# LSH attention and gMLP on one core: k of fifteen pairs turned by VectorE instead of TensorE

## The chip, the cores and the metric

The kernel runs on one core of one Trainium2 chip. The metric is the device time of one execution in microseconds (us), given as the median of several runs. The profile is of one further execution on the same chip, and its times are counted from the first instruction of the program.

## The reference

The inputs q, k and v have 4 batches, 8 heads, 768 rows and 64 columns, in float32. First comes an attention with hashed buckets: each row of q and of k gets a six-bit bucket from the signs of its product with `proj`, and a query sees only the keys of its own bucket.

```
q_bits = (einsum('bhsd,dk->bhsk', q, proj) > 0);  k_bits likewise
mask   = q_bucket[:, :, :, None] == k_bucket[:, :, None, :]
scores = where(mask, (q @ k^T) / sqrt(D), -1e9);  attn = softmax(scores)
x      = heads of (attn @ v) side by side            # 4 x 768 x 512
```

Then a gated MLP works on x: `h = gelu(x @ w_in)`, split into u and v; v is normalised, multiplied by `g_ln`, mixed over the rows by `w_sg`, and gets `b_sg` added; the output is `x + (u * v_s) @ w_out`.

## The kernel before

**The work.** The 32 heads are taken two at a time as 16 pairs, numbered n = 0 to 15. One pair needs q and k transposed: 64 columns of either head on the partitions (128 for both heads) and the 768 rows along the free dimension. Products have float32 accuracy because each operand is kept as a high part `h` (rounded to the fast format) and a low part `l` (the rest), and three products are added up: hi*hi, lo*hi and hi*lo.

**Loading and splitting a pair (what the change touches).** `load` (line 467) issues two DMAs for q and two for k on the queue of SyncE, called SP here (k of the first pair goes over ScalarE's queue). The tile has six blocks of 128 rows; a row of a head is 64 values, 256 bytes in the tile. q is loaded in blocks of 128 consecutive rows, k with six consecutive rows on each partition (`"(p t) d -> p t d"`), so the keys come in a permuted order, and `values` (line 495) loads v in the same order. The tiles for raw q and k are rings of two (`RAWS`), so that the load of a pair waits until the tile of the pair two before has been read. `parts` (line 505) then makes the transposed operands in three chunks of 512 columns, for each of which TensorE (PE in the profile) does four 128x128 transposes into PSUM (line 516), ScalarE (ACT) copies the high part (line 520) and a full copy `x` (line 529), and VectorE (DVE) subtracts the high part from PSUM to give the low part (line 523). For pair 1 alone the subtraction is done by GpSimd (POOL, line 531). A pair thus costs twelve transposes on PE, six for q and six for k.

**The rest of a pair.** `bits` (line 555) gets the sign features from `x` (PE line 563, DVE line 566, four small DMAs at line 572). `largest` (line 576) computes scores for the row maxima (PE line 591), which DVE reduces (lines 599 and 601). `shift` (line 605) carries the maxima by small DMAs into the feature tile `f` (line 618). `weigh` (line 623) computes the scores again with features and maxima (PE line 643), ACT takes the exponential (line 648), POOL adds up the row sums (line 678), and PE multiplies by v (lines 666 and 669, written `av`). `finish` (line 683) sends the sums through DRAM (lines 708 to 714), DVE inverts them on the way (line 710), and POOL and DVE scale the result (lines 721 and 722), which goes to DRAM. Beside the pairs run 16 weight jobs (line 324, DVE lines 343 to 350), which turn `w_in` into the form that the MLP needs.

**The MLP stage.** Its products are at lines 918, 1187 and 1233; on the way operands are split by ACT and by DVE or POOL (lines 895, 896, 902, 903, 1216 and 1217). Which of the two engines subtracts is listed in the constants `lox`, `loz`, `log` and `low`. `gate_raw` (line 976) and `residual` (line 1195) load in runs of 128 bytes into 32 partitions at a time and let DVE transpose 32x32 blocks (lines 984 and 986, 1203 and 1205).

**The order of the work.** Nothing is executed in the order of the source text. Every step is put into `Plan` (line 51) with an engine, an estimated cost, a priority (a due time, from constants such as `PREP`, `BITP`, `LATEQ`), and the tiles that it reads and writes. `Plan.order` simulates the engines and the SP queue with these costs and emits one fixed order; each engine, the SP queue too, then works strictly in that order. `split` (line 759) and `prepare` (line 764) place the splitting of pair n+1 some two pairs ahead of its use, and `maxima` runs `AHEAD` = 8 units ahead of `weigh` (a pair has nine units). While too little is ready at the start, PE is kept busy by 30 filler products (line 757).

Of the kernel before, what the change touches and what calls it, by code (L numbers as in the profile page):

```python
# [9 lines left out]
F32 = mybir.dt.float32  # L10
# [8 lines left out]
DRAM = bass.MemoryType.DRAM  # L19


MX = {'r0n': 3, 'zn': 2.99, 'base': 340.0, 'gs': False, 'norm': 'ACT', 'mul': ('DVE', 'DVE', 'POOL', 'DVE', 'DVE', 'POOL', 'POOL', 'DVE'), 'wg': -9.83, 'z0': -2.89, 'ox': -66.33, 'oz': -9.96, 'sp': -11.83, 'ro': -13.35, 'gr': -3.94, 'lx': 4.73, 'lz': -3.11, 'gap': 11.25, 'wo': -42.48, 'ws': 7.61, 'ul': 26.67, 'wi': -132.86, 'x0': -110.0, 'lox': ('POOL', 'DVE', 'POOL', 'POOL', 'DVE', 'DVE', 'DVE'), 'loz': ('POOL', 'DVE', 'DVE', 'DVE', 'POOL', 'POOL', 'POOL'), 'log': ('POOL', 'DVE', 'DVE', 'POOL'), 'low': ('DVE', 'DVE', 'POOL', 'DVE', 'DVE', 'DVE', 'DVE'), 'grb': 1, 'wob': 1, 'wj': -38.13}

AVP = 9.1
TRIP = 1.5
PRP, RAWS, LATEQ, PRQ = -24.5, 2, 4.39, True
GY, GX, NPT = (3,), (3, 3), 14
NAV = 1
S0P = 0.76
AHEAD = 8  # L30
PREP, SHIFTP, FINP, WSTEP, WP = 0.43, -0.07, 3.42, 14.6, 16.57
LOADS = "SP"
ADDS = (["POOL", "POOL"], ["POOL", "POOL", "POOL", "POOL", "POOL"])
TAILP = -1.15
FIRSTP, FIRSTS, FIRSTQ, LATE = -3.35, 3.76, -5.62, 11.08
LOAD0 = 1.35
PARTP = 0.39
OPS = 3
# [3 lines left out]
AHEAD1 = 2.82  # L42
LOP = (1,)
LATS, XS = (1.4, 2.6, 1.8, 3.2), 0.8
BITP, BITL, FZP, XB = -16.85, 4.0, 0.97, 1
JOB0, JOBS, JOBL = 1, 108, 6.0
LOADW = 7.8
SHIFTL = 3.2

# [1 line left out]
class Plan:  # L51
# [10 lines left out]
    TURN = 4.7  # L62
    STAY = 1.44
    BACK = 6.5
    SIDE = 1.8
    LAND = 0.62
    TAIL = {"DVE": 0.075, "ACT": 0.1, "POOL": 0.06}

    class Buf:
# [55 lines left out]
    def order(self):  # L125
# [32 lines left out]
        while len(out) < len(G):  # L158
# [44 lines left out]
            if g["dma"] and g["c"] > 1 and not g["lat"]:  # L203
                end = dma_free = max(dma_free, start + 0.6) + self.TURN
                seq[e] = max(start + 3.6, end - 1.5)
                end += 0.3 + self.LAND
                lanes.append(end + self.WAIT)
            elif g["lat"]:

                seq[e], end = end, start + g["lat"] + self.LAND  # L210
                lanes.extend([end + self.WAIT] * max(1, round(g["c"] / 0.57)))
            elif g["dma"]:
                seq[e] = end
                end = dma_free = max(dma_free, start + (1.38 if e == "ACT" else 1.3 if g["c"] > 1 else 1.2)) + g["dma"]
                end += 0.75 + self.LAND
                lanes.append(end + self.WAIT)
# [34 lines left out]
def kernel(  # L251
# [16 lines left out]
    nc = tc.nc  # L268

    B, H, S, D = q.shape  # L270
    P = 128
    NT = S // P
# [19 lines left out]
    PHASES = ((0, NY), (NY, S))  # L292
# [5 lines left out]
    ident = const.tile([P, P], F32, name="ident")  # L298
# [53 lines left out]
    PE, DVE, ACT, POOL, SP = "PE", "DVE", "ACT", "POOL", "SP"  # L352
# [4 lines left out]
    plan = Plan()  # L357
# [69 lines left out]
    if True:  # L427
# [5 lines left out]
        def ps_tile():  # L433
            ps_s.list.append(plan.slot(ps_slots, lambda i: ps_s.pool.tile([P, 512], F32, tag=f"g{i}",
                                                                          name=f"g{i}_{len(ps_s.list)}", bufs=1)))
            return ps_s.list[-1]

        def dma(prio, us, fn, r=(), w=(), e=SP, lat=0.0):
            eng = nc.sync if e == SP else nc.scalar
            plan.add(e, 0.6 if e == ACT else 0.57, prio, lambda: fn(eng), r, w, dma=us, lat=lat)  # L440
# [26 lines left out]
        def load(n, prio):  # L467
            st = Pair()
            st.n, st.b, st.hp = n, *divmod(n, NP)
            st.raw = []  # L470
            for s, (nm, src) in enumerate((("q", q), ("k", k))):
                t = early.ring([P, NT, 2, D], F32, nm, RAWS)
                for ts in ((slice(0, 2), slice(2, NT)) if n + s == 0 else (slice(0, NT),)):
                    for j in range(2):
                        def fn(eng, t=t, j=j, src=src, ts=ts):
                            order = "(p t) d -> p t d" if src is k else "(t p) d -> p t d"
                            eng.dma_start(t()[:, ts, j, :], src[st.b, 2 * st.hp + j].rearrange(order, p=P)[:, ts])
                        cost = 0.95 if s else 1.2 if n else LOAD0 * (ts.stop - ts.start) / NT
                        dma(prio + 0.2 * s + (LATEQ if ts.start else 0), cost, fn, w=[(t, (ph, j)) for ph in range(2) if ts.start <= 2 * ph < ts.stop],
                            e=ACT if n == 0 and s else LOADS)  # L480
                st.raw.append(t)
            if n == 0:
                warm = late.ring([P, 1], F32, "warm")
                plan.add(ACT, 1.4, prio + 0.5, lambda: nc.scalar.mul(warm(), small, 1.0), [], [warm])
            i = (NPAIR - 1 - n) % 3
            pool = (even, odd, early)[i]
            st.hi, st.lo = (pool.ring([P, 2, S], F32R, f"{a}{i}") for a in ("h", "l"))
            st.ft = plan.buf(f"f{i}", 1, lambda _, i=i: ftiles[i])
            pool.list.append(st.ft)
            st.x = early.ring([P, 2, S], F32, "x", XB) if n else None  # L490
            if n in (1, 2):
                plan.add(POOL, 1.5, prio + FZP, lambda t=st.ft: nc.gpsimd.memset(t().bitcast(F32), 0.0), [pnb], [st.ft])
            return st

        def values(st, prio):
            n = st.n
            st.v = pt.ring([P, 2, NT, D], F32, "v", 2)
            dma(prio + 2 if n else VP, 1.1, lambda eng: eng.dma_start(
                st.v(), v[st.b, 2 * st.hp:2 * st.hp + 2].rearrange("j (p t) d -> p j t d", t=NT)),
                r=[] if n else [(st.lo, (0, 0))], w=[st.v], e=LOADS)  # L500
        def chunk(i):
            (a, b), (c, d) = PHASES
            return ((slice(0, 2), slice(a, b), [(0, 0), (1, 0)]), (1, slice(c, d), [(1, 1)]), (0, slice(c, d), [(0, 1)]))[i]

        def parts(st, i, prio):

            hh, lo, (ss, cs, keys), tp = st.hi, st.lo, chunk(i), ps_tile()

            def at(t):
# [218 lines left out]
        sts, NPAIR = {}, B * NP  # L728
# [29 lines left out]

        def split(n, p0):
            sts[n] = load(n, p0 - (8 if n != 1 else AHEAD1))  # L760
            for i in range(3 if n else 2):
                parts(sts[n], i, p0 + 0.1 * i)

        def prepare(n):
# [30 lines left out]
        for n in range(NPAIR):  # L795
            for c in range(NU):
                if c == 0:
                    prepare(n + 1)
                g = NU * n + c
# [9 lines left out]

    M_ = MX  # L810
    V = nc.vector
# [433 lines left out]
    wi = in_weights(T + M_["wi"], T)  # L1245
# [63 lines left out]
```

## Time and profile before

| | |
|---|---|
| median of 3 runs | 699.15 us (698.44 to 699.97) |
| the profiled execution's own time | 698.67 us |
| its span, first to last instruction | 696.7 us |
| attention stage (last `av` product ends) | about 403.5 us into the span |
| MLP stage | from there to the end |
| busy: PE, DVE, ACT, POOL | 99%, 73%, 55%, 56% |

The time of a run is a little longer than the span (698.67 against 696.7 us), since starting and ending the program lie around it. PE's busy time is modelled from pipelined products, so a busy PE is one that has a product in flight. The chain of waits follows the work that ended last back through what released it. "SPq" is the queue of SyncE that issues the DMAs.

### The profile page before, as it was taken

To read this page: it belongs to the slowest core of one execution; us is meant where nothing else is said; L and a number is where in the kernel's file an instruction comes from. 1 tells how busy PE (TensorE), PEld (TensorE's weight loads), DVE (VectorE), ACT (ScalarE), POOL (GpSimd) and SP (SyncE) were. 2 spreads that over 40 slices of the span, in tenths; PEclk is the share of its full clock that TensorE was granted. 3 is DMA by queue.
4 is the path that set the end of the run, shared out by engine and by line. 5 is a ranking of instruction groups with operands and counts; after the bars stand their busy time and mean duration, and the time that the engine had idled before them with its cause. 6 is when DMAs were issued, how large, how long until landed. Compare 5 with 4: busy or idle time off the path is not lost.

```text
span 696.7 us, 16709 instructions
## 1 busy us (share of the span) xinstructions
PE 686.4 (99%) x6318; PEld 549.6 (79%) x6318; DVE 508.2 (73%) x949; ACT 380.3 (55%) x734; POOL 391.2 (56%) x346
## 2 busy tenths in 40 slices
PE   8999999999999999999999989999999999999997
PEld 8668666766766676676667579999999989899996
DVE  6878787787788769777778596786867965666343
ACT  3466666566766666676667656675774513242010
POOL 3477879777976977797679733261441514041030
PEclk9999999999999999999999999999999999999999
DMA  8524443443344334322242117888746584755433
GB/s 189 109 48 104 125 111 98 105 109 79 110 125 113 88 105 116 98 79 70 69 126 57 40 38 236 244 226 253 246 167 213 101 231 104 196 140 121 114 68 106
DMA packets 183124, 88.44 MB, mean 127 GB/s; under 512 B 148460, under 2 KB 162436, under 8 KB 183044
## 3 DMA queue, kind: packets, MB, share of 16 engines
q1 hardware_dynamic: 179940, 86.58, 46.2%
q10 hardware_dynamic: 3104, 0.80, 0.5%
q8 instruction: 50, 0.82, 0.5%
q14 instruction: 30, 0.25, 0.1%
HBM read 59.48 MB, written 25.36 MB: 122 GB/s over the span
## 4 chain that ended last, share of the span: by engine, by line
PE 91%; DMA 3%; DVE 2%; ACT 1%; issue 1%; POOL 1%; SPq 1%; ACTq 0%; DVEq 0%; POOLq 0%
PE g L643 18%; PE g L918 16%; PE g L1187 14%; PE av L666 11%; PE g L1233 9%; PE g L591 9%; PE av L669 5%; PE g L516 3%; PE g L699 2%; PE g L563 1%; PE ftp L757 1%; DMA sq<-s 1%; DMA f<-m 1%; POOL sum L678 1%; DMA r<-sq 0%
## 5 line engine op out<-in xcount | busy, mean ns | idle before, releaser
L648 ACT ACTIVATE p<-g 128x512 f32<-128x512 f32 x288 | 156.3, 599 | 60.3 <-PE g L643 58.5
L678 POOL TENSOR_TENSOR sum<-sum,p 128x512 f32<-128x512 f32 x152 | 178.3, 1206 | 3.8 <-ACT p L648 3.5
L599 DVE TENSOR_REDUCE mx<-g 128x1 f32<-128x512 f32 x192 | 123.7, 681 | 17.2 <-PE g L591 12.7
L678 POOL TENSOR_TENSOR sum<-p,p 128x512 f32<-128x512 f32 x62 | 78.9, 1295 | 42.4 <-ACT p L648 42.4
L1187 PE MATMUL g<-w,op 128*128 128x384 f32 x576 | 100.6, 334 | 0.0
L1187 PEld LDWEIGHTS g<-w,op 128*128 128x128 f32 x576 | 100.0, 188 | 0.2
L601 DVE TENSOR_REDUCE mx<-g 128x2 f32<-128x512 f32 x96 | 62.1, 684 | 43.4 <-PE g L591 41.1
L666 PE MATMUL av<-p,v 128*32 128x512 f32 x768 | 85.9, 594 | 0.0
L643 PE MATMUL g<-h 64*128 64x256 f32 (+1 forms) x384 | 70.9, 348 | 0.0
L643 PE MATMUL g<-h,l 64*128 64x256 f32 (+1 forms) x384 | 68.1, 335 | 0.0
L643 PE MATMUL g<-f 64*128 64x256 f32 (+1 forms) x384 | 67.7, 334 | 0.3 <-DMA f<-m 0.3
L591 PE MATMUL g<-f 64*128 64x512 f32 (+1 forms) x384 | 67.5, 347 | 0.0
L643 PE MATMUL g<-l,h 64*128 64x256 f32 (+1 forms) x384 | 67.5, 333 | 0.0
L591 PE MATMUL g<-h 64*128 64x512 f32 (+1 forms) x384 | 65.7, 335 | 0.0
L918 PE MATMUL g<-w,op 128*128 128x256 f32 x504 | 63.0, 287 | 2.5 <-DVE out L1071 2.5
L918 PEld LDWEIGHTS g<-w,op 128*128 128x128 f32 x504 | 62.5, 196 | 3.2 <-ACT op L895 2.8
L666 PEld LDWEIGHTS av<-p,v 128*32 128x32 f32 x768 | 23.2, 110 | 50.2 <-issue 49.3
L1233 PE MATMUL g<-woh,op 128*128 128x512 f32 x192 | 59.8, 389 | 0.0
L918 PE MATMUL g<-op,w 128*128 128x384 f32 x336 | 59.6, 335 | 0.2 <-ACT out L1068 0.2
L918 PEld LDWEIGHTS g<-op,w 128*128 128x128 f32 x336 | 58.0, 188 | 0.6 <-ACT out L1068 0.5
L721 POOL TENSOR_TENSOR xt<-un,rs 128x256 f32<-128x256 f32 (+1 forms) x32 | 34.0, 1065 | 32.9 <-DMA rs<-r 24.6
L643 PEld LDWEIGHTS g<-h 64*128 64x128 f32 x384 | 39.4, 185 | 16.4 <-DVE wflat L350 5.8
(138 smaller groups left out, 1189.6 us busy)
## 6 DMA issues: line engine op xcount, KB each, us to landing
v<-in_v_dram SPq DMA_DIRECT2D x16, 384.0 KB
raw<-xs SPq DMA_DIRECT2D x16, 384.0 KB
vn<-out SPq DMA_DIRECT2D x24, 256.0 KB
ud<-out SPq DMA_DIRECT2D x16, 384.0 KB
ul<-ud SPq DMA_DIRECT2D x32, 192.0 KB
stg<-xs SPq DMA_DIRECT2D x96, 64.0 KB
raw<-vn SPq DMA_DIRECT2D x8, 768.0 KB
out_dram<-out SPq DMA_DIRECT2D x24, 256.0 KB
```

The source lines that it names most:

```text
L591: nc.tensor.matmul(sc[j]()[:, c * NY:c * NY + b - a], x()[row(j), 0, qs], x()[row(j), 1, a:b], start=(n == 0), stop=(n == 1))
L599: nc.vector.tensor_reduce(mx()[:, 0, i0 + w, j:j + 1], sc[j]()[:, :WIDE], axis=AX.X, op=ALU.max, negate=True)
L601: nc.vector.tensor_reduce(mx()[:, 1, i0:i0 + 2, j], two(sc[j]()), axis=AX.X, op=ALU.max, negate=True)
L643: nc.tensor.matmul(sc[j]()[:, i * w:(i + 1) * w], x()[row(j), 1, ks], y()[row(j), 0, cs], start=(m == 0), stop=(m == 3))
L648: plan.add(ACT, 0.6, prio, lambda j=j: nc.scalar.activation(p[j]()[:, :, :NY], two(sc[j]()), AF.Exp, scale=SCALE), [sc[j]], [p[j]])
L666: nc.tensor.matmul(two(av())[rows(j, a)], st.v()[:, j, x, cols(a)], ps[x][j]()[:, :, :NY], start=(x == 0), stop=(x == 5))
L669: nc.tensor.matmul(av()[rows(j, a), :NY + 1], st.v()[:, j, 2 * x + i, cols(a)], ps[x][j]()[:, i, :], start=(x == 0 and i == 0), stop=(x == ...
L678: (nc.gpsimd if e == POOL else nc.vector).tensor_add(two(sums[j]()), a, p[j]()[:, :, :NY])
L721: plan.add(POOL, 0.13 + n / 420.0, prio + TAILP, lambda: nc.gpsimd.tensor_mul(xt()[:, :n], un()[:, :n], rs()[:, :n]), [un, rs], [xt])
L918: nc.tensor.matmul(ps()[:, :n], lhs(s, i, ci, x, y), rhs(s, i, ci, x, y), start=(first and ci == 0 and x + y == 0), stop=(ci == nc_ - 1 an ...
L1187: nc.tensor.matmul(ps()[:, :HN], a()[:, x, c0:c0 + P], c()[:, 3 * HN * y + ci * HN:3 * HN * y + (ci + 1) * HN], start=(j == 0 and ci == 0 ...
L1233: nc.tensor.matmul(ps(), a()[:, x, c0:c0 + P], w()[:, 2 * j + ci, :], start=(j == 1 and ci == 0 and x == 0 and w is th), stop=(j == 0 and ...
```

## The change

For pairs 1 to 15, k alone is loaded by four DMAs instead of two. Each fills 32 partitions, in runs of 32 values (128 bytes), so that VectorE can turn 32x32 blocks: one VectorE transpose writes the whole of `x` for k (128x768), ACT copies the high part from `x`, and VectorE subtracts (`turned`). q of these pairs is still transposed by PE, now in two pieces of 256 and 512 columns (`half`). All keys of these pairs come in natural order, so v is loaded in runs of one row (256 bytes). Pair 0 stays as it was. The due times and some choices of engine are other constants: among those not shown in the diff, in the table `MX`, `lox` now gives DVE, DVE, POOL, DVE, DVE, DVE, POOL (before: POOL, DVE, POOL, POOL, DVE, DVE, DVE), `log` gives four times DVE (before: POOL, DVE, DVE, POOL), `wob` is 0 (before 1), and the due times `z0`, `sp`, `ro`, `lx`, `gap`, `wo` and `x0` differ by up to some 8 units.

```diff
...
-PRP, RAWS, LATEQ, PRQ = -24.5, 2, 4.39, True
+PRP, RAWS, LATEQ, PRQ = -24.5, 2, 7.63, True
...
-PREP, SHIFTP, FINP, WSTEP, WP = 0.43, -0.07, 3.42, 14.6, 16.57
+PREP, SHIFTP, FINP, WSTEP, WP = 0.69, -0.07, 3.42, 14.6, 17.34
...
-FIRSTP, FIRSTS, FIRSTQ, LATE = -3.35, 3.76, -5.62, 11.08
+FIRSTP, FIRSTS, FIRSTQ, LATE = -3.35, 3.76, -5.55, 9.13
...
-BITP, BITL, FZP, XB = -16.85, 4.0, 0.97, 1
-JOB0, JOBS, JOBL = 1, 108, 6.0
+BITP, BITL, FZP, XB = -19.52, 4.0, 0.97, 1
+TURNED, KLO, TRP = (1,), 'DVE', 0.0
+JOB0, JOBS, JOBL = 5, 108, 6.0
...
-    SIDE = 1.8
-    LAND = 0.62
+    SIDE = 1.82
+    LAND = 0.78
...
                 t = early.ring([P, NT, 2, D], F32, nm, RAWS)
+                if n and s in TURNED:
+
+                    for g in range(4):
+                        def fn(eng, t=t, g=g, src=src):
+                            j, h = divmod(g, 2)
+                            eng.dma_start(t()[32 * g:32 * g + 32].rearrange("p t j d -> p (t j d)").rearrange("p (c d) -> p c d", d=32),
+                                          src[st.b, 2 * st.hp + j].rearrange("(c t) d -> t c d", t=32)[:, :, 32 * h:32 * h + 32])
+                        dma(prio + 0.2 * s, 1.9, fn, w=[(t, g)], e=LOADS)
+                    st.raw.append(t)
+                    continue
...
-                st.v(), v[st.b, 2 * st.hp:2 * st.hp + 2].rearrange("j (p t) d -> p j t d", t=NT)),
+                st.v(), v[st.b, 2 * st.hp:2 * st.hp + 2].rearrange("j (t p) d -> p j t d" if n and 1 in TURNED else "j (p t) d -> p j t d", t=NT)),
...
+        def turned(st, s, prio):
+            x, raw, hh, lo = st.x, st.raw[s], st.hi, st.lo
+            both = [0, 1]
+            plan.add(DVE, 0.95, prio + TRP, lambda: nc.vector.transpose(x()[:, s], raw().rearrange("p t j d -> p (t j d)")), [raw], [(x, (s, ph)) for ph in both], port=True)
+            plan.add(ACT, 0.75, prio, lambda: nc.scalar.copy(hh()[:, s], x()[:, s]), [(x, (s, ph)) for ph in both], [(hh, (s, ph)) for ph in both])
+            sub(KLO, S, prio, lambda e: e.tensor_sub(lo()[:, s], x()[:, s], hh()[:, s].bitcast(F32)),
+                [(t, (s, ph)) for t in (x, hh) for ph in both], [(lo, (s, ph)) for ph in both])
...
+        def half(st, s, ph, prio):
+
+            hh, lo, x, tp, cs, k = st.hi, st.lo, st.x, ps_tile(), slice(*PHASES[ph]), (s, ph)
+            n = cs.stop - cs.start
+
+            def tr():
+                for c in range(n // P):
+                    nc.tensor.transpose(tp()[:, c * P:(c + 1) * P], st.raw[s]()[:, cs.start // P + c].rearrange("p j d -> p (j d)"), ident)
...
+            plan.add(ACT, 0.22 + n / 1400.0, prio, lambda: nc.scalar.copy(hh()[:, s, cs], tp()[:, :n]), [tp], [(hh, k)])
+            plan.add(ACT, 0.22 + n / 1400.0, prio + 0.2, lambda: nc.scalar.copy(x()[:, s, cs], tp()[:, :n]), [tp], [(x, k)], slack=XS)
+            plan.add(DVE, 0.15 + n / 960.0, prio, lambda: nc.vector.tensor_sub(lo()[:, s, cs], tp()[:, :n], hh()[:, s, cs].bitcast(F32)), [tp, (hh, k)], [(lo, k)])
...
         def split(n, p0):
             sts[n] = load(n, p0 - (8 if n != 1 else AHEAD1))
-            for i in range(3 if n else 2):
+            if n:
+                for s in range(2):
+                    if s in TURNED:
+                        turned(sts[n], s, p0 + 0.1)
+                    else:
+                        for ph in range(2):
+                            half(sts[n], s, ph, p0 + 0.1 * ph)
+                return
+            for i in range(2):
                 parts(sts[n], i, p0 + 0.1 * i)
```

## Rows read from the trace of the kernel before

**Rows 1.** The page, busy time: engine, us, share of the span, instructions.

```profile
PE 686.4 (99%) x6318; PEld 549.6 (79%) x6318; DVE 508.2 (73%) x949; ACT 380.3 (55%) x734; POOL 391.2 (56%) x346
```

**Rows 2.** Chain of waits in order of time, one pair's length: start us, us, what.

```profile
141.51 1.46 PE g L516 x12
...
165.54 1.46 PE g L516 x12
```

**Rows 3.** Busy time by stretch; its first line names the columns.

```profile
core 0: us, PE busy (x) PEld busy (x) DVE busy (x) ACT busy (x) POOL busy (x), PEclk, DMA share, GB/s
0.00:45.00 45.00, 42.10 (x412) 33.32 (x414) 33.89 (x97) 19.28 (x38) 21.97 (x34) 1.00 0.60 128
94.00:118.00 24.00, 23.45 (x280) 15.70 (x272) 17.40 (x34) 15.37 (x31) 19.71 (x19) 1.00 0.44 114
70.00:336.00 266.00, 265.11 (x3124) 182.32 (x3116) 208.56 (x398) 172.95 (x345) 214.63 (x193) 1.00 0.38 101
412.00:415.00 3.00, 0.62 (x4) 0.30 (x2) 3.00 (x6) 2.17 (x3) 1.34 (x1) 1.00 0.10 35
415.00:419.00 4.00, 3.86 (x20) 3.89 (x21) 4.00 (x3) 3.45 (x6) 4.00 (x3) 0.60 0.26 67
430.00:490.00 60.00, 60.00 (x426) 60.00 (x425) 44.96 (x79) 38.62 (x82) 20.04 (x16) 1.00 0.84 241
```

**Rows 4.** Chain of waits in the startup: start us, us, what.

```profile
29.18 4.18 DMA f<-m
```

**Rows 5.** PE's timeline in the startup: start us, us, what, idle before.

```profile
14.35 1.95 PE L757 MATMUL ftp<-ident 128*128 128x128 f32 x16
33.40 0.73 PE L643 MATMUL g<-f 64*128 64x512 f32 x2 [0.33 <-DMA f<-m]
```

**Rows 6.** Groups by line and shape, whole span: busy us, mean ns, idle before.

```profile
L523 DVE TENSOR_TENSOR l<-g,h 128x512 fp32r<-128x512 f32 x45 | 28.4, 683 | 2.8 <-ACT x L529 2.1 <-ACT h L520 0.5
L520 ACT CAST h<-g 128x512 fp32r<-128x512 f32 x48 | 27.5, 615 | 10.0 <-PE g L516 10.0
L1034 DVE TENSOR_TENSOR out<-g,out 128x256 f32<-128x256 f32 x36 | 14.8, 420 | 9.6 <-PE g L918 5.8 <-ACT out L1031 3.9
L1216 ACT CAST op<-out 128x768 fp32r<-128x768 f32 x16 | 13.3, 836 | 54.5 <-DVE out L1155 40.1 <-POOL out L1155 14.3
L1217 DVE TENSOR_TENSOR op<-out,op 128x768 fp32r<-128x768 f32 x8 | 7.6, 951 | 2.0 <-ACT op L1216 1.9
L986 DVE STREAM_TRANSPOSE wflat<-stg 128x768 f32<-128x768 f32 x6 | 5.8, 970 | 0.9 <-DMA stg<-in_moe_w_sg_dram 0.9
```

**Rows 7.** Line 896 on DVE: count, ns min/median/max, first and last start.

```profile
L896 DVE TENSOR_TENSOR op<-raw,op x12: 918/950/2581, 399.6 to 501.3; 128x768 fp32r<-128x768 f32 x12
```

**Rows 8.** The page, DMA queue of SP and ACT: packets, MB, share of 16 engines.

```profile
q1 hardware_dynamic: 179940, 86.58, 46.2%
```

**Rows 9.** Timeline of the SP queue: start us, us, DMA, count.

```profile
166.59 0.61 SPq L477 DMA_DIRECT2D k<-in_k_dram  x1
...
170.32 2.48 SPq L618 DMA_DIRECT2D f<-m  x4
```

**Rows 10.** Line 984 on the SP queue: count, ns min/median/max, first and last start.

```profile
L984 SPq DMA_DIRECT2D stg<-in_moe_w_sg_dram x24: 332/528/4478, 430.7 to 481.5; - x24
```

**Rows 11.** PE's timeline, the first product that reads the carried maxima.

```profile
176.91 0.39 PE L643 MATMUL g<-f 64*128 64x512 f32 x2
```

**Rows 12.** Waits of the SP queue: us in total, times, longest us.

```profile
SPq L477 <- PE g L516: 25.6, 14, 4.3
```

**Rows 13.** Chain of waits in the disturbed pair: start us, us, what.

```profile
112.46 4.12 DMA sq<-s
...
116.61 0.07 DVE sq L710
...
116.70 0.67 DVE mx L599
...
117.42 1.25 PE g L516 x8
```

More of the change, by code (lines that the diff above doesn't have):

```diff
@@ L19 @@
 DRAM = bass.MemoryType.DRAM
-MX = {'r0n': 3, 'zn': 2.99, 'base': 340.0, 'gs': False, 'norm': 'ACT', 'mul': ('DVE', 'DVE', 'POOL', 'DVE', 'DVE', 'POOL', 'POOL', 'DVE'), 'wg': -9.83, 'z0': -2.89, 'ox': -66.33, 'oz': -9.96, 'sp': -11.83, 'ro': -13.35, 'gr': -3.94, 'lx': 4.73, 'lz': -3.11, 'gap': 11.25, 'wo': -42.48, 'ws': 7.61, 'ul': 26.67, 'wi': -132.86, 'x0': -110.0, 'lox': ('POOL', 'DVE', 'POOL', 'POOL', 'DVE', 'DVE', 'DVE'), 'loz': ('POOL', 'DVE', 'DVE', 'DVE', 'POOL', 'POOL', 'POOL'), 'log': ('POOL', 'DVE', 'DVE', 'POOL'), 'low': ('DVE', 'DVE', 'POOL', 'DVE', 'DVE', 'DVE', 'DVE'), 'grb': 1, 'wob': 1, 'wj': -38.13}
+MX = {'r0n': 3, 'zn': 2.99, 'base': 340.0, 'gs': False, 'norm': 'ACT', 'mul': ('DVE', 'DVE', 'POOL', 'DVE', 'DVE', 'POOL', 'POOL', 'DVE'), 'wg': -9.83, 'z0': -2.33, 'ox': -66.33, 'oz': -9.96, 'sp': -6.22, 'ro': -11.39, 'gr': -3.94, 'lx': -3.63, 'lz': -3.11, 'gap': 10.15, 'wo': -40.12, 'ws': 7.61, 'ul': 26.67, 'wi': -132.86, 'x0': -104.5, 'lox': ('DVE', 'DVE', 'POOL', 'DVE', 'DVE', 'DVE', 'POOL'), 'loz': ('POOL', 'DVE', 'DVE', 'DVE', 'POOL', 'POOL', 'POOL'), 'log': ('DVE', 'DVE', 'DVE', 'DVE'), 'low': ('DVE', 'DVE', 'POOL', 'DVE', 'DVE', 'DVE', 'DVE'), 'grb': 1, 'wob': 0, 'wj': -38.13}
 AVP = 9.1
 TRIP = 1.5
-PRP, RAWS, LATEQ, PRQ = -24.5, 2, 4.39, True
+PRP, RAWS, LATEQ, PRQ = -24.5, 2, 7.63, True
 GY, GX, NPT = (3,), (3, 3), 14
@@ L503, in chunk, with sub @@
             return ((slice(0, 2), slice(a, b), [(0, 0), (1, 0)]), (1, slice(c, d), [(1, 1)]), (0, slice(c, d), [(0, 1)]))[i]
+        def turned(st, s, prio):
[5 more added lines that the diff above has]
+                [(t, (s, ph)) for t in (x, hh) for ph in both], [(lo, (s, ph)) for ph in both])
+        def sub(e, n, prio, fn, r, w):
+            if e == POOL:
+                plan.add(POOL, 0.14 + n / 450.0, prio, lambda: fn(nc.gpsimd), r, w)
+            else:
+                plan.add(DVE, 0.15 + n / 960.0, prio, lambda: fn(nc.vector), r, w, port=True)
+        def half(st, s, ph, prio):
[4 more added lines that the diff above has]
+                    nc.tensor.transpose(tp()[:, c * P:(c + 1) * P], st.raw[s]()[:, cs.start // P + c].rearrange("p j d -> p (j d)"), ident)
+            plan.add(PE, 0.12 * n / P, prio, tr, [(st.raw[s], (h, j)) for h in range(2) for j in range(2)] + [(t, k) for t in (hh, lo)], [tp], form="full")
+            plan.add(ACT, 0.22 + n / 1400.0, prio, lambda: nc.scalar.copy(hh()[:, s, cs], tp()[:, :n]), [tp], [(hh, k)])
+            plan.add(ACT, 0.22 + n / 1400.0, prio + 0.2, lambda: nc.scalar.copy(x()[:, s, cs], tp()[:, :n]), [tp], [(x, k)], slack=XS)
+            plan.add(DVE, 0.15 + n / 960.0, prio, lambda: nc.vector.tensor_sub(lo()[:, s, cs], tp()[:, :n], hh()[:, s, cs].bitcast(F32)), [tp, (hh, k)], [(lo, k)])
         def parts(st, i, prio):
@@ L760, in split @@
             sts[n] = load(n, p0 - (8 if n != 1 else AHEAD1))
-            for i in range(3 if n else 2):
+            if n:
+                for s in range(2):
+                    if s in TURNED:
+                        turned(sts[n], s, p0 + 0.1)
+                    else:
+                        for ph in range(2):
+                            half(sts[n], s, ph, p0 + 0.1 * ph)
+                return
+            for i in range(2):
                 parts(sts[n], i, p0 + 0.1 * i)
```

## The prediction

> **What bounds the kernel now.** I read the page's busy times first: PE has a product in flight for 99% of the span, the others for 55 to 73% [rows 1]. That alone proves little, since busy time is an average over stages, so the chain of waits comes next. In a steady pair it runs through PE without a break: twelve transposes of line 516, one after another in 1.46 us, and 24.03 us later (165.54 less 141.51) the same again [rows 2]. So the pair's length is the sum of PE's work, and the transposes are 1.46 us of it, 0.122 us each. The busy times by stretch confirm it: from 70 to 336 us, 11.07 such pairs, PE is idle for 0.89 us in all, at full clock [rows 3]. DVE is busy for 208.56 us there, 18.84 a pair, POOL for 214.63, 19.39 a pair, ACT for 172.95, 15.6 a pair.
>
> Two places are not like this. At the start, 0 to 45 us, PE lacks 2.90 us and runs fillers besides [rows 3]. At the change to the MLP stage it is busy for 0.62 of 3 us while DVE works all the time; then the granted clock averages 0.60 over 4 us, that is, PE was at 1.2 GHz after this idle stretch for part of them [rows 3].
>
> **The change part by part.** *Removed from PE:* six of twelve transposes in each of pairs 1 to 15, 6 x 0.122 = 0.73 us a pair, 10.95 us for all fifteen. q's six remain one group on PE. Not every pair can give its share. Pair 1 is transposed at about 13 us, just ahead of fillers that last 1.95 us: PE has nothing to do there, so I count 0 (at most 0.73). Pair 2 is transposed at 25 us; behind it the chain leaves PE for the DMA that carries the first pair's maxima, 4.18 us from 29.18 [rows 4], and PE waits 0.33 us for it [rows 5]. That transfer doesn't wait for the transposes, so again 0 (at most 0.73). There remain pairs 3 to 15: 13 x 0.73 = **9.5 us**.
>
> *Added to DVE:* three subtractions of 512 columns go (3 x 0.683). In come two for q (256 columns 0.420, 512 columns 0.683), the 128x768 transpose (0.970), and a 128x768 subtraction from SBUF (0.951) [rows 6]: +0.97 us a pair. The same subtraction elsewhere took from 0.918 to 2.581 us [rows 7], so the upper end is +2.60. I take 0.97, because the median of those rows is 0.950. DVE then has 19.81 us (at most 21.44) in a pair of 23.30: 85% (92%). Its cover is PE's own work; if that cover were gone, the +0.97 would outweigh the 0.73.
>
> *ACT:* six copies of 512 columns (0.615 each) become two of 512, two of 256 (between half of 0.615 and the whole, 0.31 to 0.615) and one of 128x768 (0.836) [rows 6]: 3.69 becomes 2.69 to 3.30. ACT, at 15.6 of 24.03, gets relief that nothing waits for: 0.
>
> *The loads:* k has 3072 runs a pair for 1536, v 1536 for 256 or more: at most 2816 packets more. An average packet takes 46.2% x 696.7 us x 16 / 179940 = 28.6 ns of one engine [rows 8], an upper estimate for short ones, so at most 2816 x 28.6 ns / 16 = 5.0 us a pair. The DMA share would rise from 0.38 to at most 0.60 (0.38 x 24.03 + 5.0 over 23.30), and from 430 to 490 us a share of 0.84 leaves PE fully busy [rows 3]. Cost 0; lower end 0.
>
> *The SP queue:* two more issues of k a pair. Such an issue takes 0.61 us now [rows 9]; the weight load of the same shape, 32 partitions by 24 runs, took 0.528 as median [rows 10]. So +0.9 to +1.2 us a pair. What stands behind a k load in the queue are scaled results, the four DMAs that carry maxima, v, and the sign features. The four are issued from 170.32 to 172.80 [rows 9], and the first product that needs them starts at 176.91 [rows 11]: 4.1 us for a transfer whose landing in a quiet place I estimate at 2 us or less, half of the 4.18 that stood on the chain at the start [rows 4]. Some 2 us of slack take up 1.2 us: 0, at most 1.2 a pair if the slack is spent.
>
> *The moved wait:* the load of a pair waits for its raw tile, today until PE's transposes have read it, 25.6 us over 14 waits [rows 12]. Now k's tile comes free when DVE's transpose has run. If DVE is later than PE was, the SP queue stands still for that long, with the same DMAs behind it. The transpose itself reads a tile loaded most of a pair before (166.59 us in [rows 9], with the next group of transposes some 24 us after 165.54 in [rows 2]), so DVE needn't wait for it.
>
> *Startup:* pair 1's low parts leave POOL, and DVE gets 0.420 + 0.683 + 0.970 + 0.951 = 3.02 us while the first pair's maxima are reduced on it too. DVE has 33.89 of 45 us busy there, and the first fillers cover 1.95 of the 3.02. Between 0 and +3.0 I take **+0.5**, about half of the 1.07 that sticks out; also the two added issues lie ahead of v of pair 0.
>
> *The other constants:* in the MLP stage PE is busy throughout (60.00 of 60 us [rows 3]), so a subtraction moved from POOL to DVE costs 0 while DVE has 44.96 of 60. At the stage's beginning DVE is the late one [rows 3], and `lox` gives it one subtraction more: between +0.95 and a gain of 2.4 us (the idle part of 412 to 415) with 1.6 us of low clock behind it (0.40 x 4); I take 0. The due times of the weight jobs move the place where two jobs fall into one pair; the existing stalls (0.89 us) may go or grow: 0.
>
> **The sum.** -9.5 + 0.5 = -9.0 us: the span goes from 696.7 to 687.7, the profiled execution from 698.67 to 689.7. The median of the runs shown lies 0.48 above that execution, so I predict 699.15 - 9.0, in round figures **690.2 us**.
>
> **The rivals.** *A, everything gives:* pairs 1 and 2 yield their 1.46, the startup costs nothing, and the 0.89 of stalls goes: 690.2 - 1.46 - 0.5 - 0.89 = 687.3. For it: all the moved work has a pair or more of lead. Against: the startup has DVE as busy as the steady part.
>
> *B, DVE and POOL get in each other's way.* The subtraction of k reads two SBUF tiles while POOL, 83% busy over the pairs, adds. One such subtraction took 1.63 us beyond the median [rows 7], longer than it takes itself. Where two weight jobs fall into one pair (16 jobs over twelve pairs, so four pairs have a second one), DVE has no room left, and 1.63 us each would come back: 690.2 + 4 x 1.63 = 696.7. Against: POOL has 24.03 - 19.39 = 4.64 us free in a pair, into which the order can put the subtraction. The Trainium skill (SBUF — State Buffer, Who interferes with whom) says that a DVE instruction with two SBUF inputs and a GpSimd instruction that reads SBUF exclude each other, the second waiting until the first has ended; the 2.581 us row is what that would look like, and by it B would hold in every pair that has no gap on POOL, while the transpose, with one input, would wait for nobody.
>
> *C, slower: the SP queue and DVE's order.* The trace shows this mechanism once: DVE stands at the reciprocal of line 710 until a DMA round trip of 4.12 us has landed, the maxima behind it are late, and PE's transposes wait for their PSUM tile [rows 13]. PE idled 0.55 us in that stretch [rows 3]. With 1.2 us more on SP ahead of such round trips, the same could happen in every pair. It decides from 0.73 us a pair on, where it eats the whole gain. With as much as the 1.2 us in each of the 14 pairs from 2 to 15: 690.2 + 14 x 1.2 = 707.0; with 0.75, 700.7. I price it at 702, a middle value. Against: one such stall in 11 pairs, and maxima are computed eight units ahead of their use.
>
> That the change doesn't do what it says can be excluded for PE: the six instructions are gone from the order.
>
> **How the numbers follow.** My forecast 0.58 (688.6 to 692), A 0.14, B 0.13, C 0.10, and 0.05 for several small losses that end within 0.2% of before, which is about what a measurement of this kernel can tell from no change. Faster is forecast, A and B: 0.85; the same 0.05; slower 0.10. The range leaves out C and the 0.05: it goes from 686.8, just below A, to 696.8, which takes in B and with it the upper bounds of the startup (+3.0) and of the stage's beginning (+0.95).
>
> **What would show it.** Right: line 516 with 102 PE transposes for 192, its twelve of a pair become six in 0.73 us; a pair's length near 23.3 us; PE idle below 2 us from the third to the last pair; one DVE transpose of 128x768 near 0.97 us a pair; DVE at 84 to 86% there. B would show in a mean of the new subtraction well above 1 us and pairs of unequal length; C in waits of PE on DVE's maxima or on the carried maxima in most pairs, and a longer wait at line 477. I would be wrong about the whole if the pairs stayed at 24 us with PE idle in them, or if the startup (up to the first `av` product of 512 columns) came later by more than 3 us.

## The result: slower, where faster was forecast

The changed kernel takes **703.44 us** (median of 4 runs, 702.86 to 704.38), the kernel before 699.02 in the same session: ratio 1.0062, 95% interval 1.0043 to 1.0081. 690.2 us was predicted, and 703.4 lies outside the range. The profiled execution's span is 701.9 us for 696.7.

The page of the changed kernel, busy times and the queue of SP, answers to [rows 1] and [rows 8]:

```profile
PE 690.3 (98%) x6228; PEld 541.0 (77%) x6228; DVE 521.7 (74%) x979; ACT 369.1 (53%) x719; POOL 365.9 (52%) x331
...
q1 hardware_dynamic: 222660, 86.59, 50.1%
```

Busy time by stretch, the columns and stretches of [rows 3]:

```profile
core 0: us, PE busy (x) PEld busy (x) DVE busy (x) ACT busy (x) POOL busy (x), PEclk, DMA share, GB/s
0.00:45.00 45.00, 41.46 (x400) 33.30 (x404) 36.27 (x98) 19.96 (x40) 17.40 (x29) 1.00 0.61 108
70.00:336.00 266.00, 264.73 (x3010) 171.59 (x3004) 214.47 (x408) 161.36 (x327) 213.32 (x189) 1.00 0.46 101
430.00:490.00 60.00, 60.00 (x433) 60.00 (x433) 47.68 (x86) 40.18 (x87) 15.12 (x15) 1.00 0.94 261
```

Groups by line and shape: VectorE's transpose and subtraction of k, the two subtractions of q, and q's transposes on PE (with twelve of pair 0 at line 555, 102 in all for 192).

```profile
L519 DVE STREAM_TRANSPOSE x<-k 128x768 f32<-128x768 f32 x15 | 14.5, 965 | 0.0
L521 DVE TENSOR_TENSOR l<-x,h 128x768 fp32r<-128x768 f32 x15 | 14.2, 948 | 1.6 <-ACT h L520 1.6
L537 PE MATMUL g<-ident,q 128*128 128x128 f32 x90 | 13.3, 282 | 0.2 <-ACT sm L741 0.2
L542 DVE TENSOR_TENSOR l<-g,h 128x512 fp32r<-128x512 f32 x15 | 10.3, 688 | 2.7 <-ACT x L541 2.6
L542 DVE TENSOR_TENSOR l<-g,h 128x256 fp32r<-128x256 f32 x15 | 6.2, 415 | 0.0
```

Every duration is as priced, PE does 90 transposes less, and PE is still busy for 264.73 of 266 us. The time went into the attention stage: its last product with v or with the row sums starts at 408.9 us, before at 403.6 (+5.3; six products of the MLP stage, some 0.9 us, now stand ahead of it). From there to the end it is 293.0 us for 293.1.

**Where the busy row hides it.** Groups by shape, the same product of 512 columns at full clock, first before, then after:

```profile
L643 PE MATMUL g<-h 64*128 64x512 f32 x192 | 40.9, 399 | 0.0
```

```profile
L682 PE MATMUL g<-h 64*128 64x512 f32 x192 | 48.1, 417 | 1.0 <-DVE fb L605 0.3 <-DVE mx L638 0.2
```

Equal products are recorded at either about 0.39 or about 0.49 us. The long ones are the first behind a late start or behind a change of PE's tile form: 48 of the 192 after, 13 before (28 and 12 of them behind a change of form). Besides, a product lasts 0.39 us, while the next one in its rows can start after 0.23 us, so that a late start leaves no gap. One place shows it. PE's timeline of the changed kernel, then VectorE's and ACT's over the same time, and SP's (start us, us, what, idle before):

```profile
200.13 0.40 PE L630 MATMUL g<-h 64*128 64x512 f32 x2
200.37 1.07 PE L682 MATMUL g<-h 64*128 64x512 f32 x2
200.94 0.73 PE L682 MATMUL g<-h,l 64*128 64x512 f32 x2
201.28 0.62 PE L682 MATMUL g<-l,h 64*128 64x512 f32 x2
201.52 0.62 PE L682 MATMUL g<-f 64*128 64x512 f32 x2
202.05 0.39 PE L630 MATMUL g<-f 64*128 64x256 f32 x1
```

```profile
198.15 0.95 DVE L521 TENSOR_TENSOR l<-x,h 128x768 fp32r<-128x768 f32 x1
199.02 0.67 DVE L605 TENSOR_SCALAR fb<-g,fcol 128x384 fp32r<-128x384 f32 x1
199.61 1.88 DVE L638 TENSOR_REDUCE mx<-g 128x1 f32<-128x512 f32 x3
```

```profile
201.01 0.48 ACT L759 ACTIVATE g<-rs,less 128x256 f32<-128x256 f32 x1 [2.16 <-DMA rs<-r]
201.42 2.04 ACT L687 ACTIVATE p<-g 128x512 f32<-128x512 f32 x4
```

```profile
193.06 3.56 SPq L657 DMA_DIRECT2D f<-m  x4
196.72 0.54 SPq L763 DMA_DIRECT2D xs<-xt  x1
197.37 1.12 SPq L753 DMA_DIRECT2D rs<-r  x2
```

Such products start 0.23 us apart when nothing holds them (200.13 to 200.37, two heads at a time). From 200.37 to 202.05 four steps took 1.68 us: 0.76 us lost, with no idle time in the lines (the row of 1.07 us is two products, and the second starts at 200.94). By the times, that second product goes on as VectorE's second maximum ends (near 200.9), which stood behind k's subtraction and the signs; the product at 202.05 goes on as an exponential of ACT ends, which had stood behind 2.16 us of waiting for the sums `rs`, issued by SP only behind the maxima of another step. The Trainium skill (Perfetto Trace Analysis, Tensor Engine Instruction) says that a product's end is computed and not observed; durations near 0.39 or 0.49 us and little else agree.

So I counted from the starts of the products in the trace: a transpose takes 0.109 us from start to start, and 90 of them are 9.8 us. PE's tile form (64-row scores, 128x32 products with v, full transposes) changes 94 times in the attention stage before and 128 times after, in the order of the instructions. A change costs 0.15 us (measured below), 34 of them 5.1. The stage ended 5.3 us later, 0.9 of them for the six products, so the rest, 4.4 + 9.8 - 5.1 = **9.1 us**, is small waits.

The starts allow a second count, an estimate: hold each start from 45 us to the end of the stage against the earliest that the product before it in the same rows and the changes of form allow. PE then starts late by 4.4 us in all before and by 13.8 after, 9.4 more. Of these, 2.6 us end as VectorE's maxima end, 1.9 as ACT's exponentials do and 1.0 as VectorE's sign features do; 2.5 have no release near them, and the remainder is scattered. Before, q's first transposes lie 24.02 to 24.04 us apart in seven of the ten intervals from 68 to 310 us; after, the intervals there are 21.7 to 27.5 us.

### The profile page after: what moved, and what is told of

The parts are those of the page before. It is cut to its first block, busy times and chain, and to the rows that moved or that the text cites. A ratio compares the mean times of both kernels' runs of the same rounds, so it can differ in the third digit from the quotient of the medians.

```text
span 701.9 us, 16586 instructions
## 1 busy us (share of the span) xinstructions
PE 690.3 (98%) x6228; PEld 541.0 (77%) x6228; DVE 521.7 (74%) x979; ACT 369.1 (53%) x719; POOL 365.9 (52%) x331
## 5 line engine op out<-in xcount | busy, mean ns | idle before, releaser
L717 POOL TENSOR_TENSOR sum<-p,p 128x512 f32<-128x512 f32 x62 | 82.2, 1345 | 61.6 <-ACT p L687 61.5
L682 PE MATMUL g<-h 64*128 64x256 f32 (+1 forms) x384 | 81.8, 359 | 1.5 <-DVE mx L638 0.8
L682 PE MATMUL g<-h,l 64*128 64x256 f32 (+1 forms) x384 | 75.9, 339 | 0.0
L682 PE MATMUL g<-l,h 64*128 64x256 f32 (+1 forms) x384 | 74.0, 333 | 0.0
L682 PE MATMUL g<-f 64*128 64x256 f32 (+1 forms) x384 | 74.0, 333 | 0.0
L630 PE MATMUL g<-f 64*128 64x512 f32 (+1 forms) x384 | 73.3, 352 | 0.5 <-DVE mx L638 0.4
L630 PE MATMUL g<-h 64*128 64x512 f32 (+1 forms) x384 | 69.8, 336 | 0.0
L682 PEld LDWEIGHTS g<-h 64*128 64x128 f32 x384 | 44.8, 184 | 26.6 <-issue 7.9
L1202 POOL TENSOR_TENSOR out<-out,ul 128x384 f32<-128x384 f32 x12 | 13.5, 1127 | 93.2 <-DVE out L1200 70.5
```

The source lines that it names most:

```text
L630: nc.tensor.matmul(sc[j]()[:, c * NY:c * NY + b - a], x()[row(j), 0, qs], x()[row(j), 1, a:b], start=(n == 0), stop=(n == 1))
L682: nc.tensor.matmul(sc[j]()[:, i * w:(i + 1) * w], x()[row(j), 1, ks], y()[row(j), 0, cs], start=(m == 0), stop=(m == 3))
L717: (nc.gpsimd if e == POOL else nc.vector).tensor_add(two(sums[j]()), a, p[j]()[:, :, :NY])
L1202: sub(M_["mul"][2 * f + h], HN, p, lambda e: e.tensor_mul(at(f, h), at(f, h), ul()), [k, ul], [k])
```

## The experiments

Each ratio is to the kernel before, timed beside it, with its 95% interval.

**Order or constants?** First the new work in the old order (old-order run), then the new constants without the new work, the new work with the old constants, and the new code with k back on PE.

```diff
# e1_old_order: on before; k's two load steps issue two DMAs each; in the steps of k's upper chunk:
-nc.tensor.transpose(tp()[:, c:c + P], ...)            # k's six
+nc.vector.transpose(st.x()[:, 1], st.raw[1]()...)
+nc.scalar.copy(hh()[:, 1], st.x()[:, 1]); nc.vector.tensor_sub(lo()[:, 1], st.x()[:, 1], ...)
# e2_new_consts: before with the constants of after; e3_old_consts: after with those of before
# e4_not_turned: after with
-TURNED, KLO, TRP = (1,), 'DVE', 0.0
+TURNED, KLO, TRP = (), 'DVE', 0.0
```

> Edit: k of pairs 1 to 15 is loaded and turned as in the change, but every step stands where the order of the kernel before had it: the DVE transpose in the place of k's four PE transposes, the two DMAs of a head of k in the place of its one; 94 changes of PE's tile form in the attention stage, as before (the change has 128). Theory O (the order is what costs): turning saves its 10 us here, so 688 to 692 us. Theory T (the work added on DVE, the SP queue and the DMAs costs, whatever the order): 698 us or more.

> Edit: the kernel before, k on PE, with the constants (due times, engines) of the change; 116 changes of PE's form. Theory O: 22 changes of form more at some 0.19 us, 4 us, and waits of the new order of 0 to 4 us: 702 to 708. Theory T: the constants alone do nothing, 698 to 700.

> Edit: the change with the constants of before; the planner orders the new steps itself, 140 changes of PE's form. Theory O: 46 changes of form more, 9 us, against 10 us of transposes, and waits: 698 to 706, and in any case slower than the run that keeps the order of before. Theory T: as slow as the run that keeps the order of before, within 2 us.

> Edit: the change with nothing turned (its switch set to none): k by PE in pieces of 256 and 512 columns, old loads of k and v, new constants; 113 changes of PE's form. Theory O: 10 us of transposes back, fewer changes of form (-15, 3 us): 708 to 712 against 703.4 of the change. Theory T: DVE, SP and DMAs get their relief, so 698 to 702.

Measured: old order 721.11 us (1.0289, 1.0249 to 1.0329); new constants on the old code 711.05 (1.016, 1.0131 to 1.019); new code with old constants 707.01 (1.0101, 1.0067 to 1.0135); not turned 714.77 (1.0214, 1.0181 to 1.0247). So turning k is worth 11.3 us under the change's constants (714.8 to 703.4), and those constants cost the old code 12. But the old order with the new work in its places is the worst, so order and durations belong together. Both theories fell: O expected 688 to 692 us of the old-order run, and T expected 698 to 702 of the run that is not turned. The 0.19 us a change of form in these expectations was measured by no run.

**The parts, one by one, in the exact order of before.**

```diff
# e5_loads_only: k in four DMAs of 128-byte runs, v in 256-byte runs; PE transposes as before
# e6_dve_extra: behind the subtraction of k's upper chunk
+nc.vector.transpose(turned, st.raw[1]().rearrange("p t j d -> p (t j d)"))   # nobody reads it
# e7_pe_dropped: k's PE transposes left out; ACT copies and VectorE subtracts from the raw tile
-nc.vector.tensor_sub(lo()[:, ss, cs], at(tp), ...)
+nc.vector.tensor_sub(lo()[:, 1], st.raw[1]()..., ...)
# e8_dve_extra_3, e9_pe_dropped_3: the same two, and raw k in three tiles
+t.make = lambda i: early.pool.tile([P, NT, 2, D], F32, tag="k", name=f"k_{i}", bufs=3)
# e10_k_four_dmas: k in four DMAs, each over half of the partitions, runs as long as before
```

> The code and the exact order of before; of the change only the loads: k of pairs 1 to 15 comes in four DMAs of 128-byte runs, v in 256-byte runs. PE still turns k as if it lay as before, so scores and sums come from rows in another order (the products are the same in number and shape). The old-order run lost 22 us although 90 transposes were gone, and its VectorE waited 22.6 us for the sums' way through DRAM (3.5 in before). If the loads do that (they stand in SP's queue ahead of those small DMAs and share the 16 DMA engines), this run is already at 705 or more and VectorE waits over 12 us for sq. If the chain DVE, ACT, DVE of the turning does it, the loads alone cost nothing that counts: 698 to 701.

> The code, loads and exact order of before, plus one VectorE transpose of 128x768 for each of pairs 2 to 15 (14 of them) into a tile that nobody reads, right behind the subtraction of k's upper part. Nothing is taken away. 14 x 0.97 = 13.6 us of VectorE work. If VectorE time, or its quarrel with GpSimd over SBUF, is what the change pays for, this costs 4 us or more (703 and up). If VectorE has the room that its 73% suggest, 698 to 701.

> The loads and exact order of before, but k of pairs 1 to 15 is turned by nobody: ACT copies its high part and its full copy from the tile as loaded, VectorE subtracts from there (the transposition of k is left out, the number of ACT and VectorE steps stays). 90 PE transposes go and nothing comes. If PE bounds the attention stage in this order, as the prediction had it, 13 pairs x 0.73 = 9.5 us go: 688 to 692. If something else ends last once PE has less to do, at least half of that is lost: 694.5 or more.

> The run with one extra VectorE transpose per pair (734.8 us) again, in the same order, but raw k has three tiles in turn instead of two, so that the load of a pair need not wait for VectorE; the extra work is now three transposes of 128x256 into one small tile, some 1.1 us a pair. In that run SP's queue stood 54 us at the load of k for VectorE (20.8 us for PE in before), with the small DMAs of maxima, signs and sums behind it. If this stop of the queue makes the loss, the 54 us are gone and the time is 698 to 704. If VectorE's extra time or its quarrel with GpSimd makes it, 715 or more remain.

> The run without PE's transposes of k (726.6 us) again, in the same order, with three tiles of raw k in turn. There SP's queue stood 50 us at the load of k for VectorE's subtraction, which is now the last reader. If that stop was the loss, this run shows at last what 90 transposes less are worth in the order of before: 688 to 694. If the order itself cannot use a faster PE (the way of the sums through DRAM has its fixed length), 697 or more.

> The code and order of before; k of pairs 1 to 15 comes in four DMAs instead of two, each over half of the partitions, in runs as long as before; v as before. Loads alone, with short runs, cost 13.5 us. If the two more issues in SP's queue make that cost, this run is at 706 or more; if the short runs do (more than twice the packets, which the 16 engines share with the small DMAs), 698 to 702.

Measured: loads alone 713.03 us (1.0198, 1.0174 to 1.0222); one more VectorE transpose 734.80 (1.0502, 1.0476 to 1.0528); PE transposes dropped 726.60 (1.0399, 1.0363 to 1.0436), slower by 27 us with less work. Waits of the SP queue (us in total, times, longest) over the whole span tell why (the expectations count from 45 to 400 us); first the dropped transposes, then the extra one, then the extra one with a third tile:

```profile
SPq L477 <- DVE l L543: 54.7, 12, 5.4
```

```profile
SPq L478 <- DVE turned L526: 59.4, 12, 6.1
```

```profile
SPq L480 <- PE g L519: 15.1, 12, 3.6
```

The load of k waits for the raw tile's last reader, VectorE instead of PE (25.6 us in [rows 12]), and maxima, signs and sums stand behind it. With a third tile the run with the extra transposes takes 704.96 us (1.0064, 1.0046 to 1.0082), just above the 698 to 704 expected if the stop was the loss, and the one with the dropped ones 697.76 (0.9966, 0.9946 to 0.9987), in the range expected if the order cannot use a faster PE (697 or more). The stop was 29 to 30 us in both.

What stays is plain: in this order, some 15 us more on VectorE cost 4.6 us, and 9.8 us less on PE give 2.4, while PE's late starts rise from 4.4 to 12.1 us. The second isn't clean, though. Groups of that run, the subtraction that now reads two SBUF tiles, and its timeline at one place beside GpSimd's:

```profile
L545 DVE TENSOR_TENSOR l<-k,h 128x768 fp32r<-128x768 f32 x14 | 21.9, 1563 | 0.0
```

```profile
169.22 2.50 DVE L545 TENSOR_TENSOR l<-k,h 128x768 fp32r<-128x768 f32 x1
...
166.83 3.50 POOL L710 TENSOR_TENSOR sum<-sum,p 128x512 f32<-128x512 f32 x3
```

It takes until GpSimd's sums have ended (170.33) and 1.4 us more; its mean is 1.563 us for the 0.948 in the changed kernel, where the planner keeps it clear of GpSimd's work (`port=True` in the diff). VectorE has 1.563 + 0.677 + 0.420 us a pair for 3 x 0.683 there, +0.61; at the price of the extra transposes (4.6 us for some 1.1 a pair) that is about 2.6 us, so without it the dropped transposes would be worth about 5, by this estimate, and not 9.5.

With four DMAs for k in long runs the kernel takes 709.38 us (1.0137, 1.0096 to 1.0178), so some 9 of the loads' 13.4 us go with the two issues. VectorE's wait for the sums' way through DRAM, from 70 to 336 us, before and in that run:

```profile
DVE sq L710 <- DMA sq<-s: 3.5, 6, 1.1
```

```profile
DVE sq L715 <- DMA sq<-s: 18.2, 17, 2.0
```

The maxima stand behind this wait, and PE starts late by 14.5 us there (4.4 before), 11.0 of them (1.6) until maxima end.

The parts found in this order, 13.4 + 4.6 - 2.4 = 15.6 us, make most of the 21.8 that the old-order run lost. The rest was not settled; k's subtraction took 1.353 us there for the 0.948 of the changed kernel.

**The parts, one by one, in the exact order of after.**

```diff
# f1_long_runs: k in two DMAs in long runs (in the places of the first and third), v as before
# f3_q_dropped: q's PE transposes left out too; ACT and VectorE read raw q, which has three tiles
# f5_dve_dropped: VectorE's transpose left out; ACT, VectorE and the sign product read raw k, three tiles
# h6_all_undone: f1 and f5 together
# h1_no_trip_wait:
-V.reciprocal(sq()[:, :W], sq()[:, :W])
+V.reciprocal(sr()[:, :W], sqc[:, :W])          # sqc: a constant
# g1_turned_tuned: other due times, penalties and MLP engines; among them
-    STAY = 1.44
+    STAY = 7.956
-AVP = 9.1
+AVP = 12.72
```

> The code and exact order of after, but k of pairs 1 to 15 is loaded as before (two DMAs in long runs, in the places of the first and third of the four) and v as before; VectorE turns what then lies there, so the result is of other rows. In the order of before the four DMAs in short runs cost 13.5 us (two more issues alone 9 us). If SP's queue is what the changed kernel pays for in its own order too, 4 us or more go: 699.5 or less. If the order of after was laid out round the four issues, it has paid already and nothing comes back: 701 to 705.

> The code, loads and exact order of after, but q of pairs 1 to 15 is turned by nobody either: ACT copies and VectorE subtracts from the tile as loaded, which has three tiles in turn so that its load need not wait for them. Left out are 90 more PE transposes (0.73 us a pair, 10.9 us in all) and the changes of form round them. If PE still bounds the attention stage, 693 or less. If the stage now ends by other chains (sums through DRAM and SP's queue, VectorE's maxima), most of it is lost: 698 or more.

> The code, loads and exact order of after, but VectorE's transpose is left out: ACT, VectorE's subtraction and the sign product take k from the tile as loaded, which has three tiles in turn. 15 x 0.97 = 14.6 us of VectorE work go. One extra transpose a pair cost 4.6 us in the order of before with three tiles. If VectorE's work is a cost of its own here too, 3 us or more go: 700 or less; if VectorE has room in this order, 701 to 705.

> The code of after with other constants for due times, penalties and the choice of engines in the MLP, so another order of the same work: 112 changes of form on PE in the attention stage instead of 128 (94 before), same loads, same transposes on VectorE. If the order is the loss, 2 us of form changes and some of the waits go: 694 to 699, level with before or better. If the added work is the loss whatever the order, 701 or more.

> The code, loads and exact order of after, but VectorE takes the reciprocal of a constant tile instead of the sums that came back from DRAM, so neither VectorE nor SP's queue waits for that way in its place; all DMAs are still issued. The scale of the result is left out. VectorE stood 13.6 us for those sums between 70 and 336 us (3.5 in before) and the row maxima stand behind it. If this wait is what the changed order loses by, 3 us or more go: 700 or less. If the loss is spread over many waits, 701 to 704.

> The exact order of after with everything undone that the change added: long loads in two DMAs (-3.2 us alone) and no VectorE transpose (-1.2 us alone), with three tiles of raw k; the 90 PE transposes of k stay away. k is turned by nobody. If the added work is the loss, this shows the gain that the prediction had priced: 690 to 694. If the order itself is, the parts only add up to 698 to 700.5, level with before, although PE does 9.8 us less.

Measured: long loads 700.27 us (1.002, 1.0008 to 1.0032), 3.2 less than the changed kernel; no VectorE transpose 702.20 (1.005, 1.0035 to 1.0065), 1.2 less; no wait for the sums 702.10 (1.0042, 1.0021 to 1.0063), 1.3 less, though VectorE had stood 13.6 us there; the other order 702.02 (1.004, 1.0025 to 1.0056), 1.4 less with 112 changes of form. q's transposes dropped as well gave 702.76 (1.0052, 1.0035 to 1.0069): 0.7, but VectorE's subtraction of q's 512 columns then took 1.247 us for 0.688, so this run says less than it was meant to. By their intervals only the long loads differ from the changed kernel (1.0043 to 1.0081); the other four could be no change. The long loads fell between the expected ranges. The other order, by its expectation, spoke for the added work as the loss; it only shows that fewer changes of form alone do not make an order good.

Everything undone is the decisive one: **699.26 us** (1.0008, 0.9995 to 1.0022), inside the 698 to 700.5 expected if the order is the loss. With the added loads and VectorE's transpose gone and 90 transposes fewer on PE, the order of after is level with before; PE's late starts are 8.8 us for 4.4. VectorE's subtractions of a pair take 1.030 + 0.689 + 0.415 us there for 3 x 0.683, so they are hardly the reason. The two parts add up: 3.2 + 1.2 = 4.4 alone, 4.2 together.

**The price of a change of form, and the stop in before.**

```diff
# h7_form_changes: on before, in weigh, between the two key tiles of a step of 256 queries
+if i:
+    nc.tensor.transpose(sc[0]()[:, w:w + P], ident, ident)
# h5_before_3_raw: before, raw k in three tiles, nothing else
```

> The code and order of before, with one 128x128 transpose of the identity put between the two key tiles of each score step of 256 queries (48 of them), into the part of PSUM that the second tile then overwrites: PE goes from its 64-row form to the 128-row form and back. Bare, 48 x 0.109 = 5.2 us; with two changes of form each at the 0.10 us that the starts of the products suggest, 9.6 us more. If a change of form costs that, and PE's order has no room, 711 to 715; if changes are free, 702 to 705.

> The code and exact order of before with three tiles of raw k in turn instead of two, nothing else. SP's queue stood 20.8 us (11 times) at a load for PE's transposes in before, and with a later release of the tile this stop cost 29 us. If the stop already costs before something, 1 to 2 us go: 697 to 698.5. If it lies in slack there, 699 to 700.

Form changes: 717.77 us against 698.15 (1.0282, 1.0263 to 1.0301), +19.6, more than expected. PE's timeline round one of them:

```profile
183.12 0.28 PE L645 MATMUL g<-l,h 64*128 64x256 f32 x2
183.24 0.28 PE L645 MATMUL g<-f 64*128 64x256 f32 x2
183.45 0.33 PE L642 MATMUL g<-ident 128*128 128x128 f32 x1
183.70 0.39 PE L645 MATMUL g<-h 64*128 64x256 f32 x2
183.93 0.28 PE L645 MATMUL g<-h,l 64*128 64x256 f32 x2
```

Undisturbed, these start 0.12 us apart. From 183.24 to 183.93 it is 0.69 for two steps: 0.45 for the detour, 0.11 of them the transpose. By the whole time (19.6 - 48 x 0.109) / 96 = 0.15 us a change. The starts in the traces of the two kernels say it kind by kind. PE's timeline of before, behind a change from 128x32 products:

```profile
124.97 0.38 PE L643 MATMUL g<-h 64*128 64x256 f32 x2
125.19 0.28 PE L643 MATMUL g<-h,l 64*128 64x256 f32 x2
125.31 0.28 PE L643 MATMUL g<-l,h 64*128 64x256 f32 x2
```

The step across a change is 0.09 us longer than one within a form. Behind a change to 64-row products the next step is 0.10 longer too (0.22 here, then 0.12), behind one to full transposes 0.055. So the three kinds cost 0.20 (to 64 rows), 0.15 (to full) and 0.09 us (to 128x32), and the 34 more changes, 17, 1 and 16 of them, 5.0 us.

Before with a third raw tile: 697.99 us against 699.05 (0.9982, 0.9967 to 0.9998), the one version that does all the work and is below both kernels, if by 1 us. Held against this run, which has the third tile too, the dropped PE transposes are worth 1.1 us by the ratios (0.9966 and 0.9982), which the intervals cannot tell from nothing, and the extra VectorE transposes cost 5.7. SP's stop there fell from 25.6 to 15.2 us:

```profile
SPq L479 <- PE g L518: 15.2, 12, 3.6
```

## Why the prediction was wrong

**The step that failed** is the passage "the other constants": "the existing stalls (0.89 us) may go or grow: 0", and under it the sentence that "the pair's length is the sum of PE's work". I took PE's 265.11 of 266 us for a proof that PE alone sets the pair's length and that the 0.73 a pair would come off any order. The busy row cannot show that: with 90 transposes dropped it still said 262.51 of 266 in the old order, and the kernel was 2.4 us faster, not 9.5. What the runs put in its place, against before:

| | us | shown by |
|---|---|---|
| 90 transposes off PE | -9.8 | starts of the products |
| 34 more changes of form | +5.1 | 0.15 each, the form run; 5.0 by the starts |
| more small waits, from the order and the new cut of the steps | +4.9 | what is left with everything undone (699.26 against 699.05) |
| loads of k and v | +3.2 | long loads |
| VectorE's transpose | +1.2 | transpose dropped, not clear of noise |
| sum | +4.6 | +4.4 measured |

The waits add up to 9.3 us by these medians, to 9.1 in the profiled execution and to 9.4 by the late starts. The third line is a remainder of +4.9 (+4.4 by the late starts): which constant of the order makes it was not settled. Taking the wait for the sums away gave back only 1.3 us by the medians, so that wait alone is not the loss.

*Removed from PE.* The count was right (192 to 102), and 9.5 against 9.8 in size; that it would reach the end was the error above.

*Added to VectorE.* 0.965 + 0.948 + 0.688 + 0.415 - 3 x 0.683 = +0.97 us a pair, as priced. "Its cover is PE's own work" nearly held: 1.2 us, within the noise.

*The loads* and *the SP queue* at 0: wrong together by 3.2 us. The two weren't separated in the order of after; in that of before the issues were the larger part, 9 of 13.4, where the prediction's upper end, 1.2 us a pair, would be 16.8 for 14 pairs. The DMA share of 0.46 was within the bound of 0.60; that the queue cost here and not the engines is likely by this, but not shown.

*The moved wait* at 0: right in the changed kernel, where the load of k hardly ever waits for VectorE (7.0 us of waits for PE at q's loads lead there). In the old order, where VectorE read the tile late, with the extra transpose or in place of PE, it cost 29 to 30 us; in the old-order run itself the queue stood 21.8 us for it, no longer than for PE before (25.6). The prediction named the wait and had no row for its size.

*Startup:* the first product with v starts at 26.23 us for 26.40, but the first of 512 columns, which the prediction had named as the sign, at 44.60 for 38.89. That is the order and not a loss: with each product but transposes and fillers counted at its step (an estimate from the starts), the changed kernel has done by 51.3 us what the one before has by 51.4. It is 0.3 us behind at 186 us and 4.7 at 355, so the loss comes in the later pairs. *MLP:* 293.0 us for 293.1, as good as 0.

**Rivals.** A did not come. B is real but was avoided: the subtraction took 1.35 us in the old-order run and 1.563 in the run above, and 0.948 in the changed kernel. The Trainium skill (SBUF — State Buffer, Who interferes with whom) says that of a VectorE instruction with two SBUF inputs and a GpSimd instruction that reads SBUF the second waits until the first has ended; the 2.50 us row agrees, since it does not end before GpSimd's sums do. C came nearest, at 702, and names the right places (VectorE's wait for `sq` rose from 3.5 to 13.6 us), but they are a part of the loss only: 2.6 of the 9.4 us of late starts end with maxima.

The signs I had named failed too. PE's idle time stayed below 2 us (1.27), which was to speak for the forecast; VectorE was at 81%, not 84 to 86, because the pairs had not become shorter. The pairs did stay near 24 us, a sign named against the forecast, but without the idle time that was to go with it.

## What to carry to other kernels

A busy share near 100% on PE says that products are in flight, not that the time falls with the work; compare the starts of equal products before counting a gain. In a fixed order, price the order too: count the changes of PE's tile form in it, the issues on each in-order DMA queue, and who is the last reader of each buffer that a load refills. When work moves to another engine, give the refilled buffer one more tile before the order is changed; here that alone was worth 29 to 30 us where VectorE read the tile late, and 1 us in the kernel as it stood.

## What the hardware showed that I had not expected

A change of PE's tile form costs 0.15 us in the mean, more than one transpose (0.109), and shows as busy time. The Trainium skill (TensorEngine Tiling (Array Packing), Key Properties) says that changing the tiling mode drains TensorE, and gives no figure; the form run agrees. Two more DMA issues a pair on the SP queue, with the bytes and runs unchanged, cost 9 us in 15 pairs; small DMAs on the way of the sums and maxima stand behind them, and VectorE's wait for the sums rose from 3.5 to 18.2 us. And dropping 90 instructions from PE, with VectorE instead of PE as the last reader of raw k, made the kernel 27 us slower, until a buffer was added.
